# Two attention blocks side by side: 64-key half blocks, pads from the projection, and three relays through DRAM

## The chip, the cores and the metric

The kernel runs on one core of one Trainium2 chip. The metric is the device time of one execution, in microseconds (us). A program on one core has no second die to compare with, so "fast" here means within 1.5% of the fastest execution of the same kernel. The times are medians of all four executions of a run; four of these runs hold one slow execution (370.15, 420.29, 314.03 and 340.23 us; their fast executions alone give 369.87, 419.18, 313.94 and 339.91).

The profile's names: PE is TensorE (matmuls), PEld its weight loads, DVE is VectorE, ACT ScalarE, POOL GpSimd; SP is the engine that issues transfers (DMAs). PSUM is the memory that the matmuls of these kernels write to. The granted clock is the share of TensorE's full clock in the records.

## The reference

Two independent blocks of S = 2048 rows, D = 640, 32 heads of 20 columns. Block A is causal attention over a window of 256 keys. Block B is linear attention.

```python
qkv = (x @ wqkv).reshape(B, S, 3, H, Dh)...          # A
scores = einsum("bhqd,bhkd->bhqk", q, k) * Dh ** -0.5
mask = (i - j >= 0) & (i - j < 256)
a = softmax(where(mask, scores, -1e9)) @ v  -> @ wo
phi = lambda t: where(t > 0, t + 1, exp(t)) + 1e-6   # B
kv, z = phi(k)^T v, sum(phi(k))
b = (phi(q) kv) / (phi(q) z + 1e-6)  -> @ wo
return concatenate([a, b], axis=-1)                  # [1, 2048, 1280]
```

## The kernel before

A small planner in Python orders all operations by estimated times and emits them engine by engine. The order is then fixed. The SP queue issues nearly all transfers, in order.

A head has 20 columns, and the kernel gives each head a group of 32 rows (a pad). The old kernel projects 128 columns at a time, copies them to a stage, and moves each head's rows to its 32-row pad with a DMA of its own:

```python
def em(e, c=c):                                     # in proj_pad, for q and for k
    ...
    for h, r0, cnt, d0 in head_pieces[c]:           # 36 pieces per 512 queries
        hg, j = divmod(h, 4)
        nc.sync.dma_start(out=box["t"][32*j+d0 : 32*j+d0+cnt, hg, :],
                          in_=st["t"][r0 : r0+cnt, c, :])
```

One attention unit is 128 queries of 4 heads against 3 key blocks of 128. It takes 12 score matmuls, two exponentials, a mask multiply, and 12 matmuls in which the probabilities are stationary and 21 columns (20 values and a 1) move. The denominators come out in column 21, one per query, so VectorE divides with queries on the partitions, without any transfer:

```python
nc.vector.reciprocal(out=r[:], in_=O[:, :, Dh:HV])
nc.vector.tensor_tensor(out=otok..., in0=O[:, :, 0:Dh], in1=r[:].to_broadcast([P, 16, Dh]), op=ALU.mult)
```

Five transposes on TensorE then put the head columns on the partitions for the output projection.

The softmax here doesn't subtract the row's maximum and nothing guards it: scores larger than these inputs give would overflow.

Of the kernel before, what the change touches and what calls it, by code (L numbers as in the profile page):

```python
# [15 lines left out]
class Op:  # L16


    __slots__ = ("engs", "emit", "key", "left", "ready", "end", "succ", "lat", "group", "first", "last", "name")

    def __init__(self, engs, emit, key, lat, earliest):
        self.engs = engs
        self.emit = emit
        self.key = key
        self.lat = lat
        self.left = 0
        self.ready = earliest
        self.end = None
        self.succ = []
        self.group = None  # L30
        self.first = False
        self.last = False
        self.name = ""


class Planner:


    LAT = {"PE": 0.25, "ACT": 0.12, "DVE": 0.12, "POOL": 0.15, "SP": 2.2, "ACTQ": 2.2}

    def __init__(self, fill_bufs):
        self.avail = {}
        self.free = {}
        self.fill_bufs = fill_bufs
        self.fill_end = [0.0] * fill_bufs
        self.groups_open = 0
        self.n_groups = 0
        self.log = []

    def op(self, engs, emit, key, deps=(), lat=None, earliest=0.0, group=None, name=""):  # L50
        o = Op(engs, emit, key, lat, earliest)
        o.name = name or ".".join(emit.__qualname__.split(".<locals>.")[1:])
        o.group = group
        for d in deps:
            if d is None:
                continue
            if d.end is None:
                d.succ.append(o)
                o.left += 1
            else:  # L60
                o.ready = max(o.ready, d.end)
        if o.left == 0:
            self._push(o)
        return o

    def _push(self, o):
        for e in o.engs:
            self.avail.setdefault(e, []).append(o)

    def _start_time(self, o):  # L70
        if o.group is not None and o.first:
            return max(o.ready, self.fill_end[self.n_groups % self.fill_bufs])
        return o.ready

    def run(self):
        while True:
            best = None
            for e, ops in self.avail.items():
# [3 lines left out]
                t0 = INF  # L82
                for o in ops:
                    s = self._start_time(o)
                    if s < t0:
                        t0 = s
                if t0 == INF:
                    continue
                t = max(f, t0)
                pick = None  # L90
                for o in ops:
                    if self._start_time(o) <= t + 1e-9:
                        k = (o.key, o.ready)
                        if pick is None or k < pick[0]:
                            pick = (k, o)
                if best is None or t < best[0]:
                    best = (t, e, pick[1])
# [6 lines left out]
            if o.group is not None and o.first:  # L104
                slot = self.n_groups % self.fill_bufs
                o.group["slot"] = slot
                self.fill_end[slot] = INF
                self.n_groups += 1
# [4 lines left out]
            if o.group is not None and o.last:  # L113
                self.fill_end[o.group["slot"]] = o.end
# [5 lines left out]
        assert not any(self.avail.values())  # L120


def act_t(n):
    return 0.075 + 0.000833 * n


def dve_ps(n):
    return 0.07 + 0.00104 * n
# [11 lines left out]
def kernel(  # L140
# [14 lines left out]
    HD = 32  # L155
    HV = Dh + 1
    HG = H // 4
    KT = D // P
    NT = S // P
    NQ = 512  # L160
    NTT = S // NQ
    TB = NQ // P
    HALF = D // 2
    scale = float(Dh) ** -0.5
    out2 = out[0]
    xA = A_x[0]
    xB = B_x[0]
    PACE = 2.0
    EVK = -4000

    ctx.enter_context(tc.manual_schedule())
    pl = Planner(2)

    def pool(name, bufs, **kw):
        return ctx.enter_context(tc.tile_pool(name=name, bufs=bufs, **kw))

    PS = bass.MemoryType.PSUM
    const = pool("const", 1)
    wpool = pool("w", 1)
    xpool = pool("x", 4)  # L180
    stage_pool = pool("stage", 2)
    qpool = pool("q", 2)
    kpool = pool("k", 3)
    vpool = pool("v", 9)
    ppool = pool("p", 4)
    small = pool("small", 2)
    epool = pool("e", 3)
    opool = pool("o", 3)
    over = pool("over", 1)
    dram = pool("dram", 1, space=bass.MemoryType.DRAM)  # L190
    s3pool = pool("s3", 1, space=PS)
    s1pool = pool("s1", 2, space=PS)
    accpool = pool("acc", 1, space=PS)
    fpool = pool("fill", 2, space=PS)


    warm = const.tile([P, NQ], BF16, name="warm")
    nc.vector.memset(warm[:], 0.0)
    tiny = const.tile([P, 1], F32, name="tiny")
    nc.vector.memset(tiny[:], 1e-6)  # L200
    tinyo = const.tile([P, 1], F32, name="tinyo")
    nc.scalar.activation(out=tinyo[:], in_=tiny[:], func=ACT.Exp)
    ones = const.tile([P, 1], BF16, name="ones")
    nc.vector.memset(ones[:], 1.0)


    wA = [wpool.tile([P, KT, D], BF16, name=f"wA{i}") for i in range(3)]
    woA = wpool.tile([P, KT, D], BF16, name="woA")
    wkqB = pool("wkqB", 1)
    wvB = wpool.tile([P, KT, D], BF16, name="wvB")  # L210
    wo6 = wpool.tile([120, 6, D], BF16, name="wo6")
    wAv = A_wqkv.rearrange("(kt p) n -> p kt n", p=P)
    wBv = B_wqkv.rearrange("(kt p) n -> p kt n", p=P)

    MB = 1.0 / 0.2

    def dma(eng, emit, mbytes, key, deps=(), n=1, lat=2.2, name=""):
        return pl.op({eng: max(0.07 * n, mbytes * MB)}, emit, key, deps, lat=lat, name=name)

    def q_of(e):  # L220
        return nc.sync if e == "SP" else nc.scalar

    class Fifo:


        def __init__(self, n):
            self.n = n
            self.users = []

        def need(self):  # L230
            return self.users[-self.n] if len(self.users) >= self.n else []

        def add(self, ops):
            self.users.append(ops)


    x_users = Fifo(4)
    x_tiles = {}

    def load_x(which, t, key):  # L240
        src = (xA if which == "A" else xB).rearrange("s (c p) -> s c p", p=P)
        box = {}

        def emit(e, box=box):
            box["t"] = xpool.tile([P, KT, NQ], BF16, name="xT")
            for c in range(KT):
                nc.sync.dma_start_transpose(out=box["t"][:, c, :], in_=src[t * NQ : (t + 1) * NQ, c, :])  # L247

        o = dma("SP", emit, 0.655, key, deps=x_users.need(), n=5)
        box["op"] = o  # L250
        box["users"] = []
        x_users.add(box["users"])
        x_tiles[(which, t)] = box
        return box

    def load_w(eng, dst, src, key, mb=0.82, deps=()):
        return dma(eng, lambda e: q_of(eng).dma_start(out=dst, in_=src), mb, key, deps)


    def group(mms, evac, key, deps=(), shape=None, dtype=F32, chunk=2, name=""):  # L260

        g = {}
        name = name or mms[0][1].__qualname__.split(".<locals>.")[1]
        prev = None
        n = len(mms)
        i = 0
        first = True
        while i < n:
            part = mms[i : i + chunk]

            def emit(e, part=part, first=first):
                if first:
                    g["ps"] = fpool.tile(shape or [P, NQ], dtype, name="F")
                for _, m in part:
                    m(g["ps"])

            o = pl.op({"PE": sum(m[0] for m in part)}, emit, key if first else -1000, list(deps) if first else [prev], lat=0.0 if i + chunk < n else None, group=g, name=name)
            o.first = first
            if first:
                g["first"] = o  # L280
            prev = o
            first = False
            i += chunk
        g["mm"] = prev
        last = prev
        res = []
        for engs, em in evac:
            o = pl.op(engs, (lambda e, em=em: em(g["ps"], e)), EVK, [last], name=name)
            last = o
            res.append(o)  # L290
        last.group = g
        last.last = True
        g["ev"] = res
        g["end"] = last
        return g

    def copy_to(dst):
        def em(ps, e, dst=dst):
            d, s = dst(ps)
            if e == "ACT":  # L300
                nc.scalar.copy(out=d, in_=s)
            else:
                nc.vector.tensor_copy(out=d, in_=s)  # L303
        return em

    def either(n, act=True):
        d = {"DVE": dve_ps(n)}
        if act:
            d["ACT"] = act_t(n)
        return d  # L310

    head_pieces = []
    for c in range(KT):
        pieces = []
# [565 lines left out]
```

## Time and profile before

| | before |
|---|---|
| median of 3 runs before the prediction | 454.76 us |
| TensorE (PE) busy | 325.0 us, 72% |
| VectorE / ScalarE busy | 240.8 / 213.7 us |
| first score matmul | 67.55 us |
| pad transfers issued | 288 |

The first and fourth parts of the page follow: busy time by engine, then the shares of the chain of waits that ended last (SPq is the queue of SP; L370 is the pad transfer above).

```profile
span 452.2 us, 10028 instructions
PE 325.0 (72%) x4184; PEld 190.4 (42%) x4216; DVE 240.8 (53%) x478; ACT 213.7 (47%) x334; POOL 11.4 (3%) x36
...
PE 41%; SPq 22%; DVE 18%; ACT 7%; DMA 7%; issue 5%; DVEq 0%; ACTq 0%
```

The timeline at the start: start, duration, engine, line, operation, how many; in brackets, the idle time before it and what ended it.

```profile
15.29 27.67 SPq L370 DMA_DIRECT2D qpad<-stage  x36
...
43.06 16.34 SPq L370 DMA_DIRECT2D kpad<-stage  x22
...
64.80 2.83 PE L588 MATMUL F<-wkq,xT 128*128 128x320 bf16 x10 [35.50 <-DMA kpad<-stage]
```

An issue costs about 0.77 us (27.67 us for 36). All engines stand for 35 us behind the queue, and smaller holes of this kind follow at each new slice of 512 queries.

### The profile page before, as it was taken

The numbers are of one execution on the slowest core, as the hardware profiler recorded it, in microseconds if no ns is written. First come the engines' busy times: TensorE is split into PE (matmuls) and PEld (weight loads), VectorE is DVE, ScalarE is ACT, GpSimd is POOL, SyncE is SP. The second block draws the span as 40 slices with busy tenths as digits, with TensorE's granted clock in tenths as the row PEclk, the third lists the DMA queues.
The fourth block names the chain that finished last, engine by engine and source line by source line (L and its number), as shares of the span: only waits on it lengthen the run. The fifth ranks groups of instructions, "written<-read, shape, count | busy, mean of one in ns | idle before, by whom it ended". The sixth has DMA issues, their size and how long they took to land.

```text
span 452.2 us, 10028 instructions
## 1 busy us (share of the span) xinstructions
PE 325.0 (72%) x4184; PEld 190.4 (42%) x4216; DVE 240.8 (53%) x478; ACT 213.7 (47%) x334; POOL 11.4 (3%) x36
## 2 busy tenths in 40 slices
PE   5950025699945758899985789998771788797856
PEld 1430013255522426575653557545340444454523
DVE  0540006278742418766542437767741379779674
ACT  1000005288944539977102557898140598596020
POOL 4000000000000000000000005000000000000000
PEclk9895558599995559998996969699895799699898
DMA  9511133825254223370213133043111400010101
GB/s 217 130 25 24 25 95 74 150 55 105 50 154 91 50 54 79 64 141 20 66 27 81 25 86 64 2 105 97 39 26 36 111 15 16 17 61 17 58 30 58
DMA packets 62335, 29.82 MB, mean 66 GB/s; under 512 B 46546, under 2 KB 62162, under 8 KB 62290
## 3 DMA queue, kind: packets, MB, share of 16 engines
q1 hardware_dynamic: 60322, 27.55, 25.7%
q10 hardware_dynamic: 1968, 1.64, 1.2%
q8 instruction: 33, 0.54, 0.5%
q14 instruction: 12, 0.10, 0.1%
HBM read 9.99 MB, written 6.06 MB: 36 GB/s over the span
## 4 chain that ended last, share of the span: by engine, by line
PE 41%; SPq 22%; DVE 18%; ACT 7%; DMA 7%; issue 5%; DVEq 0%; ACTq 0%
SPq L370 17%; PE F L541 9%; PE F L346 7%; PE O L486 5%; PE F L620 5%; SPq L247 5%; DVE p L472 4%; DMA kpad<-stage 4%; ACT p L461 4%; PE F L388 3%; DVE rB L760 3%; DMA xT<-in_A_x_dram 2%; PE F L733 2%; DVE pq L575 2%; PE F L588 2%
## 5 line engine op out<-in xcount | busy, mean ns | idle before, releaser
L472 DVE TENSOR_TENSOR p<-p,maskED 128x1024 bf16<-128x1024 bf16 x112 | 77.4, 697 | 22.4 <-ACT p L464 21.9
L486 PEld LDWEIGHTS <-p 128*128 128x128 bf16 x1440 | 51.6, 98 | 32.1 <-DVE p L472 14.8
L486 PE MATMUL O<-v,p 128*128 128x21 bf16 x1440 | 57.2, 175 | 10.3 <-DVE p L472 6.6
L588 PE MATMUL F<-wkq,xT 128*128 128x320 bf16 x160 | 33.9, 341 | 36.7 <-DMA kpad<-stage 35.5
L444 PEld LDWEIGHTS <-kpad 20*128 20x128 bf16 x1440 | 25.6, 96 | 64.0 <-DMA kpad<-stage 32.6
L541 PE MATMUL F<-kvwo,pq 128*128 128x320 bf16 x160 | 32.4, 356 | 21.3 <-DVE osb L550 12.1
L550 DVE CAST osb<-F 128x320 bf16<-128x320 f32 x56 | 27.3, 489 | 35.0 <-PE F L541 17.6
L356 DVE CAST stage<-F 128x512 bf16<-128x512 f32 x32 | 22.1, 690 | 34.1 <-PE F L346 31.8
L346 PE MATMUL F<-xT,wA_115 128*128 128x512 bf16 x88 | 29.4, 442 | 14.2 <-DMA xT<-in_A_x_dram 12.3
L388 PE MATMUL F<-wA_117,xT 128*128 128x320 bf16 x160 | 33.3, 335 | 2.4 <-DVE osb L550 1.9
L588 PEld LDWEIGHTS <-xT 128*128 128x128 bf16 x160 | 15.3, 107 | 45.6 <-DMA kpad<-stage 35.8
L541 PEld LDWEIGHTS <-pq 128*128 128x128 bf16 x160 | 17.1, 112 | 33.0 <-issue 15.5
L541 PE MATMUL F<-woA,oT 128*128 128x320 bf16 x160 | 30.5, 316 | 0.3
L567 ACT ACTIVATE e_401<-F 128x320 bf16<-128x320 f32 x1 | 0.4, 437 | 64.0 <-PE F L588 64.0
L620 PE MATMUL F<-pk,xtok 128*128 128x320 bf16 x160 | 28.5, 316 | 0.0
L733 PE MATMUL F<-xT,wqp 128*128 128x512 bf16 x91 | 25.0, 383 | 4.0 <-DVE pq L575 2.9
L346 PE MATMUL F<-xT,wA_116 128*128 128x512 bf16 x91 | 24.0, 390 | 0.7 <-DVE GT L303 0.4
L400 DVE CAST v<-F 128x320 bf16<-128x320 f32 x28 | 13.8, 492 | 16.8 <-PE F L388 16.7
L388 PEld LDWEIGHTS <-xT 128*128 128x128 bf16 x160 | 15.5, 105 | 10.6 <-issue 2.9
L572 DVE TENSOR_SCALAR e_406<-e_401 128x320 bf16<-128x320 bf16 x1 | 0.2, 244 | 37.0 <-ACT e_401 L567 37.0
L346 PEld LDWEIGHTS <-wA_115 128*128 128x128 bf16 x100 | 9.3, 106 | 22.2 <-issue 11.8
L620 PEld LDWEIGHTS <-xtok 128*128 128x128 bf16 x160 | 14.8, 102 | 7.5 <-issue 0.2
(721 smaller groups left out, 537.1 us busy)
## 6 DMA issues: line engine op xcount, KB each, us to landing
out_dram<-osb SPq DMA_DIRECT2D x32, 160.0 KB
xtok<-in_B_x_dram SPq DMA_DIRECT2D x5, 512.0 KB
qpad<-stage SPq DMA_DIRECT2D x112, 20.0 KB
kpad<-stage SPq DMA_DIRECT2D x112, 20.0 KB
wkq<-in_B_wqkv_dram SPq DMA_DIRECT2D x2, 800.0 KB
wA_116<-in_A_wqkv_dram ACTq DMA_DIRECT2D x1, 800.0 KB
wA_117<-in_A_wqkv_dram SPq DMA_DIRECT2D x1, 800.0 KB
woA<-in_A_wo_dram SPq DMA_DIRECT2D x1, 800.0 KB
```

The costliest lines, as they stand in the source:

```text
L247: nc.sync.dma_start_transpose(out=box["t"][:, c, :], in_=src[t * NQ : (t + 1) * NQ, c, :])
L346: nc.tensor.matmul(ps[:], lhsT=wA[i][:, kt, c * P : (c + 1) * P], rhs=xb["t"][:, kt, :], start=(kt == 0), stop=(kt == KT - 1))
L370: nc.sync.dma_start(out=box["t"][HD * j + d0 : HD * j + d0 + cnt, hg, :], in_=st["t"][r0 : r0 + cnt, c, :])
L388: nc.tensor.matmul(ps[:], lhsT=xb["t"][:, kt, b * P : (b + 1) * P], rhs=wA[2][:, kt, hf * HALF : (hf + 1) * HALF], start=(kt == 0), stop=( ...
L444: nc.tensor.matmul(o, lhsT=kt_[HD * j : HD * j + Dh, hg, ko : ko + P], rhs=qbox["t"][HD * j : HD * j + Dh, hg, b * P : (b + 1) * P], start ...
L472: nc.vector.tensor_tensor(out=p[:, :, 0:3:2, :], in0=p[:, :, 0:3:2, :], in1=maskED[:, None, :, :].to_broadcast([P, 4, 2, P]), op=ALU.mult)
L486: nc.tensor.matmul(O[:, hh0 + j, 0:HV], lhsT=st["p"][:, j, i, :], rhs=vA[kb]["t"][:, hg * 4 + j, :], start=(i == idx0), stop=(i == 2))
L541: return lambda ps: nc.tensor.matmul(ps[:], lhsT=lhs(c), rhs=rhs(c, hf), start=(c == 0), stop=(c == KT - 1))
L550: nc.vector.tensor_copy(out=d, in_=ps[:])
L588: return lambda ps: nc.tensor.matmul(ps[:], lhsT=xb["t"][:, kt, b * P : (b + 1) * P], rhs=R["wk"][:, kt, hf * HALF : (hf + 1) * HALF], sta ...
L620: return lambda ps: nc.tensor.matmul(ps[:], lhsT=box["t"][:, tb, :], rhs=R["pk", tb // TB][:, tb % TB, hf * HALF : (hf + 1) * HALF], start ...
L733: return lambda ps: nc.tensor.matmul(ps[:], lhsT=R["wqp"][:, kt, c, :], rhs=xb["t"][:, kt, :], start=(kt == 0), stop=(kt == KT - 1))
```

## The change

The intent is to remove the pad DMAs and to make the attention cheaper:

- The weight columns are reordered on VectorE so that the projection gives 20 heads directly in 32-row pads. The 12 spare rows of each pad carry the columns of the other 12 heads, which are relaid through DRAM: 10 writes and 6 reads of 512 KB.
- Scores use 64-key halves with shifted query ranges, so that less masked-out work is done: 78 units of 2048 columns with one exponential each.
- The values become the stationary operand in 64x32 tiles, so the results have head columns on the partitions and need no transpose. The denominators now lie in one row per head. They go to DRAM, back as 128x32 for the reciprocal, to DRAM again, and back broadcast to 32 rows per head. Heads are then relaid through DRAM for the output projection.
- The planner is rewritten: PSUM banks by a common pool, scores paced, its own estimates of durations.

The core of the diff, cut; planner, pools, block B and the order of calls are left out:

```diff
-                for h, r0, cnt, d0 in head_pieces[c]:
-                    nc.sync.dma_start(out=box["t"][HD*j+d0 : HD*j+d0+cnt, hg, :], in_=st["t"][r0:r0+cnt, c, :])
+    def relay_write(m, tt, key):
+        dst = DQK[tt][0 : 32 * NH, :].rearrange("(r b) n -> b r n", b=NH)[4 * m : 4 * m + 4, :, :]
+        dma("SP", lambda q: q.dma_start(out=dst, in_=QK[m][:, c0 : c0 + RW]), 0.52, ...)
+    def relay_read(g, tt, key):
+        src = bass.AP(..., ap=[[NH * RW, 4], [RW, 32], [1, RW]])
+        dma("SP", lambda q: q.dma_start(out=QK[g][:, c0 : c0 + RW], in_=src), 0.52, ...)
 ...
-                    nc.tensor.matmul(O[:, hh0 + j, 0:HV], lhsT=st["p"][:, j, i, :], rhs=vA[kb]["t"][:, hg * 4 + j, :], ...)
+                        nc.tensor.matmul(FB[box[rg]][32*j : 32*j+32, qc : qc+w], lhsT=V[...][64*rho : 64*rho+64, HV*h : HV*h+32],
+                                         rhs=PT[u % NP][64*rho : 64*rho+64, j, cc : cc+w], ..., tile_position=(64*rho, 32*j))
 ...
-                nc.vector.reciprocal(out=r[:], in_=O[:, :, Dh:HV])
+        dma("SP", lambda q: q.dma_start(out=d1[:], in_=ON[nb][Dh : Dh + 97 : 32, :]), ...)
+        dma("SP", lambda q: q.dma_start(out=RC[nb][:], in_=d1[:].rearrange("a (b c) -> (a b) c", c=32)), ...)
+        pl.op({"DVE": 0.35}, lambda e: nc.vector.reciprocal(out=RD[nb][:], in_=RC[nb][:]), ...)
+        dma("SP", lambda q: q.dma_start(out=d2[:].rearrange("a (b c) -> (a b) c", c=32), in_=RD[nb][:]), ...)
+        dma("SP", lambda q: q.dma_start(out=RB[nb][:], in_=d2[:, None, :].to_broadcast([4, 32, TQ])), 0.3, ..., lat=2.6)
+        # OS = ON * RB on VectorE, then:
+            dst = DO[tt][:].rearrange("(r b) n -> b r n", b=32)[4 * g : 4 * g + 4, :, :]     # g < 5
+            dst = DO[tt][o : o + P, :]                                                         # g >= 5
+        dma("SP", lambda q: q.dma_start(out=dst, in_=os_[:]), 0.26, ...)
+            src = DO[tt][:].rearrange("(r b) n -> b r n", b=32)[4 * m : 4 * m + 4, :, :]
+            dma("SP", lambda q, m=m, src=src: q.dma_start(out=OT[:, m, :], in_=src), 0.26, ...)
```

## The prediction

> **What bounds the kernel now.** The span is 452.2 us (the page's first part) with PE busy 325.0 (72%), DVE 240.8, ACT 213.7. In a table of 10 us windows PE is busy 9 to 9.9 of 10 wherever it is fed (90 to 120, 190 to 230, 270 to 310); the other 127 us are holes. The largest is 29.9 to 64.8: no compute engine works, and the list of waits gives PE 35.5 us on the last kpad transfer. The chain of waits gives 22% to the SP queue, 17% of it the line that relays heads into 32-row pads. The timeline shows why: 36 such issues last 27.67 us, 0.77 each, and there are 288 (DMA issues: 224 full pieces, 64 part pieces), about 220 us of one in-order queue. Holes at 130 to 170, 230 to 270 and 330 to 360 end on the same transfers. So: SP issues at each new 512-query slice, otherwise PE.
>
> **Removed.** The 288 pad issues. 128 score units with two exponentials each (1.13 us for 1152 columns, 0.48 for 384: about 196 us of ACT). Attention on PE: scores about 50 us, values 57 us busy (group table). Mask multiplies 77.4+6.5 us DVE, transposes 7.3 PE and 7.7 DVE, four wide reciprocals 13.4.
>
> **Added or moved.** 78 units of 2048 columns: the slope of the measured exponentials (0.84 ns a column) gives 1.88 us each, 147 in all. Masks shrink to 61,440 columns, about 40 us. I count 1600 score and 2144 value matmuls, in 32x64 and 64x32 tiles. Today's 12 four-tile score matmuls start within 0.14 us and the next full-array one 0.14 us after the last of them; this agrees with the Trainium skill, "TensorEngine Tiling (Array Packing)", Key Properties: tiles run in parallel, a change of mode drains the array. At about 16 ns per matmul plus some 190 mode changes at 0.1 us I estimate 60 to 70 us of attention on PE, 40 less than now. ACT and DVE gain copies (B's projections before phi, 32 of 512 columns for the value sums) and 32 normalisations of about 0.6 us. DMA grows from 29.8 to about 47 MB (pads through DRAM 8.4, reciprocals broadcast 8.4, heads through DRAM 5.2), with five dependent SP issues for each of 16 head groups, each link about 2 us (a pad lands in 1.9 today).
>
> **On the critical path.** PE work becomes about 278 us. At today's share where fed, 0.92, that is 302; a start of about 12 without the pad stall and a tail of about 8 (last denominators, rows and store) give about 320. ACT and DVE need about 195 us each if shared evenly, so they do not bound.
>
> **Predicted: 318 us, 8 times in 10 between 288 and 362.** Faster by over 2%: 0.96; within 2%: 0.02; slower: 0.02.
>
> **Signs.** Right if: no hole over 10 us after the first 20; first score unit before 20 us; PE busy 260 to 295 us and over 80% of the span; exponentials about 1.88 us x78; SP queue under 10% of the chain; granted clock above 0.9 (holes show 0.5). Wrong if PE busy stays above 310 (small tiles issue slower than 16 ns), or SP waits on its own DRAM round trips dominate.
>
> **What could make it wrong.** Head-of-line blocking in SP: transposing loads still take 1.26 us each, 60 of them, and denominator round trips wait in the same queue. If landing takes 4 us rather than 2 the plan slips, and 350 or more is likely. If the new schedule fits the engines' true times well, 290.

## The result, and the profile after

The changed kernel takes 471.34 us (median of 4 runs, 469.85 to 471.66), the old one 455.44 in the same rounds. The ratio is 1.035, 95% interval 1.030 to 1.040: slower. Ratios here are the mean time of one kernel's fast runs over that of the other's in the same rounds, so they are not quite the ratio of the medians.

The same parts of the page after the change (the second line of shares goes by source line), and the line of its DMA part for the SP queue:

```profile
span 470.0 us, 11365 instructions
PE 305.6 (65%) x5000; PEld 166.6 (35%) x5000; DVE 221.4 (47%) x442; ACT 191.5 (41%) x168; POOL 128.8 (27%) x155
...
q1 hardware_dynamic: 60858, 40.97, 54.2%
...
DMA 53%; PE 19%; DVE 12%; SPq 10%; issue 4%; ACT 1%; POOL 0%; POOLq 0%; DVEq 0%; ACTq 0%
DMA RB<-d 22%; DMA RC<-d 8%; DMA d<-RD 8%; SPq L355 7%; DMA d<-ON 6%; PE F L657 3%; PE F L622 3%; PE F L424 3%; DVE OS L602 3%; DMA OT<-do 3%; DMA do<-OS 3%; PE F L394 3%; PE F L726 2%; PE SC L483 2%; PE F L572 2%
```

Three engines have less work, as intended: PE 19 us less, VectorE 19, ScalarE 22. (GpSimd has 117 us more, since it takes most of the masks.) But transfers hold 53% of the chain where they held 7%. The broadcast of the reciprocals (RB<-d) alone has 22%, and the four links of the denominators together about 43%. The list of waits for VectorE says the same: engine, tile, line, what it waited for; total, times, longest.

```profile
DVE OS L602 <- DMA RB<-d: 97.8, 13, 21.9
DVE RD L596 <- DMA RC<-d: 36.9, 9, 10.4
```

How that stops everything is seen in the timeline at 300 us:

```profile
299.77 1.15 SPq L598 DMA_DIRECT2D RB<-d  x1
300.97 5.33 SPq L355 DMA_TRANSPOSE X<-in_B_x_dram  x1
306.35 0.57 SPq L594 DMA_DIRECT2D d<-ON  x1
314.61 0.69 DVE L602 TENSOR_TENSOR OS<-ON,RB 128x512 bf16<-128x512 f32 x1 [21.86 <-DMA RB<-d]
315.22 0.68 DVE L317 CAST R<-F 128x512 bf16<-128x512 f32 x1
...
315.94 0.63 ACT L648 ACTIVATE E<-R 128x512 bf16<-128x512 bf16 x1 [20.24 <-DVE R L317]
315.96 0.58 PE L726 MATMUL F<-X,XT 128*128 128x512 bf16 x1 [21.30 <-DVE R L317]
```

The broadcast is issued at 299.77 and VectorE starts on it at 314.61. In the planned order of VectorE the normalisation stands in front of the copy that frees a PSUM bank (R<-F), and VectorE starts that copy only afterwards. So ScalarE and PE wait for a transfer that neither of them reads. The table of windows shows two stretches of 10 us without any work (busy time of PE, weight loads, VectorE, ScalarE and GpSimd, then granted clock, share of the 16 DMA engines, GB/s):

```profile
110.00:120.00 10.00, 0.00 (x0) 0.00 (x0) 0.00 (x0) 0.00 (x0) 0.00 (x0) 0.50 0.94 97
...
300.00:310.00 10.00, 0.00 (x0) 0.00 (x0) 0.00 (x0) 0.00 (x0) 0.00 (x0) 0.50 0.89 116
```

The share of 0.94 does not mean that 16 engines moved data. It adds up the durations of packets, the parts of a transfer that the trace records. In the first of these stretches 26 of 1908 packets took over 0.5 us each and hold 95.7 of the 150.5 us; 22 of the 26 are of 256 bytes or less, and the usual packet of 256 bytes takes 18 ns. So that time was waiting for the most part.

Why does a transfer of 512 KB take so long? The trace records every update of a semaphore by a DMA. The Trainium skill ("DMA: Bandwidth & Descriptors", Why a DMA increments its semaphore by 16 and not by 1) says that a transfer from the SP queue runs on k of 16 DMA engines, k being the largest number up to 16 that divides the outermost dimension (the slowest one that is not 1) on both sides. By the same section each of the k engines posts one update, and the issuer posts the rest at once. The count of updates per transfer therefore tells k: 16 for k = 16, otherwise k + 1. Counted from the records of the changed kernel (landing is from the end of issue to the last update, the median of the transfers whose records are complete):

```
transfer                       size     x    updates  engines  landing, median us
RB<-d    broadcast             512 KB   16   5        4        8.7
dqk<-QK  pad relay, write      512 KB   10   5        4        10.5
QK<-dqk  pad relay, read       512 KB    6   5        4        14.7
OT<-do   head relay, read      256 KB   10   5        4        9.0
do<-OS   head relay, g < 5     256 KB   10   5        4        6.5
do<-OS   head relay, g >= 5    256 KB    6   16       16       2.1
out      stores (POOL queue)   160 KB   32   16       16       1.5 to 2.3
X<-B_x   transposing loads               40   16       16       5.7  (2.1 in the old kernel)
```

A few transfers lack an update or more in the records; the counts are the usual ones. In the old kernel pads of 20 rows show 11 updates, so 10 engines. The packets say the same without the rule: for most of the time in which a broadcast moves, exactly four of its packets of 4 KB are in flight, 159 ns each. So 128 packets need about 5.1 us on four engines (an estimate), and the fastest broadcasts land in 7.4.

The page also says that it is always the lowest-numbered k engines. If that holds, 22 of the 50.3 MB (16, 10 and 6 times 512 KB, 20 times 256 KB) go through the same 4 engines, which also carry their share of everything else. At 4 KB in 159 ns these 22 MB alone keep four engines busy for about 213 us (an estimate).

**Theory A:** the outermost dimension of 4 confines these transfers to 4 engines, which clogs them for all other traffic; the dependent denominators then wait in that jam. **Rival B:** the number of dependent round trips in one in-order queue costs the time, whatever their bytes. **Rival C:** a large transfer by itself, or reading the same DRAM rows 32 times, is slow.

### The profile page after: what moved, and what is told of

The parts are those of the page before. It is cut to its first block, busy times and chain, and to the rows that moved or that the text cites. A ratio compares the mean times of both kernels' runs of the same rounds, so it can differ in the third digit from the quotient of the medians.

```text
span 470.0 us, 11365 instructions
## 1 busy us (share of the span) xinstructions
PE 305.6 (65%) x5000; PEld 166.6 (35%) x5000; DVE 221.4 (47%) x442; ACT 191.5 (41%) x168; POOL 128.8 (27%) x155
## 4 chain that ended last, share of the span: by engine, by line
DMA 53%; PE 19%; DVE 12%; SPq 10%; issue 4%; ACT 1%; POOL 0%; POOLq 0%; DVEq 0%; ACTq 0%
DMA RB<-d 22%; DMA RC<-d 8%; DMA d<-RD 8%; SPq L355 7%; DMA d<-ON 6%; PE F L657 3%; PE F L622 3%; PE F L424 3%; DVE OS L602 3%; DMA OT<-do 3%; DMA do<-OS 3%; PE F L394 3%; PE F L726 2%; PE SC L483 2%; PE F L572 2%
## 5 line engine op out<-in xcount | busy, mean ns | idle before, releaser
L490 ACT ACTIVATE P<-SC 128x2048 bf16<-128x2048 f32 x78 | 146.4, 1877 | 144.9 <-PE SC L483 143.7
L513 POOL TENSOR_TENSOR P<-P,MK 128x512 bf16<-128x512 bf16 (+1 forms) x94 | 99.7, 1068 | 276.2 <-ACT P L490 272.0
L602 DVE TENSOR_TENSOR OS<-ON,RB 128x512 bf16<-128x512 f32 x32 | 23.2, 744 | 102.0 <-DMA RB<-d 97.8
L657 PE MATMUL F<-W,X 128*128 128x320 bf16 x160 | 30.5, 343 | 41.1 <-DVE R L317 36.8
L726 PE MATMUL F<-X,XT 128*128 128x512 bf16 x100 | 28.5, 424 | 27.4 <-DVE R L317 24.1
L572 PE MATMUL F<-P,V 64*32 64x64 bf16 (+4 forms) x2144 | 31.8, 254 | 21.2 <-issue 13.1
L622 PE MATMUL F<-W,OT 128*128 128x320 bf16 x160 | 30.1, 340 | 22.6 <-DMA OT<-do 16.0
L483 PE MATMUL SC<-QK 20*64 20x128 bf16 (+4 forms) x1600 | 36.6, 272 | 4.8 <-ACT P L490 3.1
L317 DVE CAST R<-F 128x320 bf16<-128x320 f32 (+1 forms) x55 | 28.2, 521 | 13.1 <-PE F L622 5.6
L666 PE MATMUL F<-R,XT 128*128 128x320 bf16 x160 | 27.2, 321 | 1.6 <-DVE ON L317 1.6
L513 DVE TENSOR_TENSOR P<-P,MK 128x512 bf16<-128x512 bf16 (+1 forms) x54 | 25.7, 482 | 3.7 <-ACT P L490 3.4
```

The source lines that it names most:

```text
L317: nc.vector.tensor_copy(out=dst, in_=src)
L483: nc.tensor.matmul(SC[64 * rho : 64 * rho + 64, j, cc : cc + w], lhsT=QK[g][32 * j : 32 * j + Dh, kc : kc + 64], rhs=QK[g][32 * j : 32 * j ...
L490: nc.scalar.activation(out=pt[:], in_=SC[:], func=ACT.Exp, scale=scale)
L513: eng.tensor_tensor(out=pt[:, :, cc : cc + w], in0=pt[:, :, cc : cc + w], in1=MK[:, None, lo:hi].to_broadcast([P, 4, w]), op=ALU.mult)
L572: nc.tensor.matmul(FB[box[rg]][32 * j : 32 * j + 32, qc : qc + w], lhsT=V[kb % NV][64 * rho : 64 * rho + 64, HV * h : HV * h + 32], rhs=PT ...
L602: pl.op({"DVE": dve_ps(NX)}, lambda e, c=c: nc.vector.tensor_tensor(out=os_[:, c], in0=ON[nb][:, c], in1=RB[nb][:, c], op=ALU.mult), -2900 ...
```

## The experiments

Eleven experiments in twelve runs, each timed in rounds with the old kernel. The changed kernel is the base unless said otherwise.

### All five kinds on 16 engines

Each transfer is cut into four of 32 rows. Bytes and planned order stay.

```diff
-q.dma_start(out=RB[nb][:], in_=d2[:, None, :].to_broadcast([4, 32, TQ]))
+for j in range(4):
+    q.dma_start(out=RB[nb][32*j : 32*j+32, :], in_=d2[j : j+1, :].to_broadcast([32, TQ]))
-q.dma_start(out=dst, in_=QK[m][:, c0 : c0 + RW])
+for j in range(4):
+    q.dma_start(out=dst[j], in_=QK[m][32*j : 32*j+32, c0 : c0 + RW])
 # and likewise QK<-dqk, do<-OS for g < 5, OT<-do
```

> Same plan and same bytes as the changed kernel; each transfer whose outermost dimension is 4 (reciprocal broadcast, pad relay both ways, head relay both ways) is cut into four of 32 rows. Theory A (those transfers run on 4 of the 16 engines and clog them for all others): every one now shows all engines, the 512 KB broadcast lands in about 3 us after its issue instead of 8.7, span 300 to 350 us. Rival B (the dependent chain of round trips in one in-order queue costs, whatever the bytes): 150 more issues at 0.5 us in that queue, span unchanged or worse, 460 to 500 us.

370.15 us, ratio to the old kernel 0.815 (0.809 to 0.820), result correct. Rival B falls as the reason for these 100 us, since there are more issues and the same links; what the links cost with all engines is measured further below. A's number was missed: 370 is outside 300 to 350. One of the four executions, the profiled one, took 1340 us (see the last section), so the kernel was run again.

> The kernel with all transfers on 16 engines once more, because the profile of its first run fell in an execution of 1340 us with matmuls four times as long. 368 to 372 us, and a usable profile: PE busy about 305 us, no hole over 10 us after the first 30.

369.52 us, ratio 0.814. The shares of the chain, first by engine and then by line:

```profile
span 369.0 us, 11580 instructions
...
PE 32%; DVE 24%; DMA 21%; SPq 14%; issue 5%; ACT 2%; POOL 0%; DVEq 0%; POOLq 0%; ACTq 0%
DMA RB<-d 9%; PE F L394 7%; PE F L432 5%; SPq L355 5%; DVE OS L614 5%; PE F L680 4%; SPq L608 4%; PE F L645 4%; PE SC L491 3%; DVE R L673 3%; DMA RC<-d 3%; PE F L580 3%; DVE R L317 3%; DVE P L521 3%; SPq L634 3%
```

Each piece now shows 16 updates, and up to about 16 packets of the broadcast are in flight. One piece of it (128 KB) lands in 2.6 us. The whole broadcast, from the end of its first issue to the landing of its fourth piece, takes 4.3 us (was 8.7) and not the 3 expected; the pad relays take 4.5 and 5.0 (10.5 and 14.7). Five head reads together take 11.6 us where they took 15.6: their 20 pieces land 0.45 us apart, and one issue takes 0.42. The transposing loads of block B, which the edit does not touch, land in 1.6 us (5.7): they had been waiting behind the others. PE busy was expected at about 305 us; it is 282.2 in this profile. "No hole over 10 us" was just missed: PE has one of 10.7 us at 230 us.

### One part at a time

> Only the broadcast of the reciprocals is cut into four of 32 rows; the relays stay on 4 engines. A: broadcast lands in 3 to 5 us, about half of the gain of the run with all cut, span 370 to 420 us, since 13.6 MB still go through 4 engines. B: unchanged, 465 to 480.

Only the broadcast cut by rows: 431.88 us, ratio 0.952, a gain of 39 us and less than expected. The whole broadcast lands in 5.0 us (median), at the end of what was expected. But the relays are still on 4 engines (the pad relays land in 9.7 and 15.3 us), and other links land later than with all cut (d<-RD in 2.7 us, not 1.1).

> The reverse: pad and head relays are cut into 32 rows, the broadcast stays on 4 engines (8.4 MB). A: x transposes land faster (median 5.7 us falls towards 2.1), broadcast alone takes about 8 us still, span 390 to 430 us. B: unchanged or worse, 465 to 490.

Only the relays cut: 412.52 us, ratio 0.910, a gain of 59 us. Transposing loads land in 2.4 us, the broadcast still takes 8.2. The two gains add up to 98 us; both cuts together give 101. (The old kernel's medians in the rounds of these runs, 452.39 to 455.44 us, allow such differences to within some 3 us.)

### Controls for the cut itself

```diff
+for j in range(4):                                       # e4: by columns, outermost still 4
+    q.dma_start(out=RB[nb][:, 256*j : 256*j+256], in_=d2[:, None, 256*j : 256*j+256].to_broadcast([4, 32, 256]))
+for j in range(2):                                       # e9: by rows, outermost 2
+    q.dma_start(out=RB[nb][64*j : 64*j+64, :], in_=d2[2*j : 2*j+2, None, :].to_broadcast([2, 32, TQ]))
```

> Control: the broadcast is cut into four DMAs by columns, each still with an outermost dimension of 4, so the same number of issues as the row cut but the same 4 engines. A: no gain, 465 to 490 us, last piece lands as late as before. A rival C, that one large DMA is slow and several in flight are faster, expects the gain of the row cut here too (under 430).

475.58 us, ratio 1.046: no gain from the cut as such, although four transfers are in flight. Each piece shows 5 updates. The pieces land one after the other, 1.4 us apart, and the last comes 8.6 us after the end of the first issue (one broadcast: 8.7).

> The changed kernel with the broadcast cut into two DMAs whose outermost dimension is 2: 256 KB each, same bytes. Theory A in its sharp form (the outermost dimension sets how many engines a transfer gets, and they are the same few each time): 2 engines, 3 updates per landing, 512 KB land in about 16 us after issue, span clearly longer than 471, 530 to 620 us. Rival (a transfer is slow because it is large, or because it reads the same DRAM rows 32 times): no longer than the changed kernel, 455 to 480.

547.47 us, ratio 1.203. Each piece shows 3 updates, so 2 engines. While both pieces are under way mostly two packets are in flight, not four, and the second lands 5.0 us (median) after the first: both go through the same two engines. The broadcast takes more of the chain than in any other run:

```profile
span 547.4 us, 11386 instructions
...
DMA 57%; PE 17%; issue 8%; SPq 8%; DVE 8%; ACT 1%; POOL 0%; POOLq 0%; DVEq 0%
DMA RB<-d 30%; DMA d<-RD 8%; DMA d<-ON 6%; DMA RC<-d 5%; SPq L355 4%; PE F L394 3%; DVE OS L606 3%; DMA OT<-do 2%; PE F L626 2%; PE F L661 2%; PE F L424 2%; PE SC L483 2%; PE F L572 2%; SPq L600 2%; DMA W<-in_A_wo_dram 1%
```

The same bytes in smaller transfers cost 76 us more. Rival C falls with these two: size and repeated reads are as before, or smaller. The sharp form of A stands, the outermost dimension setting the engines. The landing of 16 us after the issue was an overestimate: both pieces together take 13.3 us (median of 16; 11.8 to 19.0).

### The same links without the bytes

```diff
-q.dma_start(out=RB[nb][:], in_=d2[:, None, :].to_broadcast([4, 32, TQ]))
+q.dma_start(out=RB[nb][0:P:32, :], in_=d2[:])            # wrong result on purpose
```

> Wrong result on purpose. In the changed kernel as it is, the broadcast moves only the 4 rows of 4 KB and not their 32 copies: all five dependent links, the issues and the plan stay, 8.1 MB on 4 engines go. Theory A: 425 to 440 us, as with the broadcast on 16 engines (432). Rival B (number of links): no change, 465 to 475.

420.29 us, ratio 0.925. The links, the issues and the plan are unchanged, and 51 us go with the 8.1 MB. This is a little more than expected, and 12 us more than when the broadcast runs on all engines.

### What remained: the plan and the chain

370 is still 52 us over the prediction. Two candidates: the planner believes that a cut transfer takes one issue when it takes four (`n=4` corrects it), or the chain of the denominators itself.

> The same, and the planner is told that these transfers take four issues each, so that it orders the SP queue by their true cost. If what is left over 318 us is an in-order queue that runs late against its plan, 345 to 362 us. If the queue is no longer the limit, 366 to 374.

350.63 us, ratio 0.771: the true issue counts were worth 19 us. The normalisations' waits for the broadcast, 97.8 us in the changed kernel and 38.5 with all engines, are gone from the list of waits.

> Wrong result on purpose. With all transfers on 16 engines, the denominator chain of the 16 head groups is taken out: the normalisation multiplies by ones that were set at the start. What is left of the chain's latency and of its SP waits goes away. If the remaining 50 us over my prediction are that chain: 315 to 335 us. If they are PE work, masks and copies: 355 to 368.

314.03 us, ratio 0.691 (wrong result), just under the first case. Against 369.5 with the same issue estimates, the chain costs 55 us, with all engines at work. But leaving out operations also lets the planner order the rest anew, so the test was repeated with the informed plan.

> Wrong result on purpose. The chain is taken out of the version with all engines and the informed plan (350.6 us), so that both sides of the comparison order their queue with true issue counts. If the chain itself costs about 36 us there, 308 to 318 us. If the informed plan had already hidden most of it and the earlier run without a chain gained by a luckier order, 325 to 345.

318.22 us, ratio 0.699 (wrong result), at the upper edge of the first case. So with true issue counts the chain costs 32 us (350.6 to 318.2), what the planner gains by its absence included, and without it the true counts are worth nothing (314 and 318). The page's first part of the informed plan, and then of the same without the chain:

```profile
span 348.4 us, 11567 instructions
PE 279.5 (80%) x5000; PEld 160.4 (46%) x5000; DVE 238.0 (68%) x457; ACT 189.2 (54%) x164; POOL 117.9 (34%) x144
```

```profile
span 315.8 us, 11364 instructions
PE 267.8 (85%) x5000; PEld 154.1 (49%) x5000; DVE 234.5 (74%) x444; ACT 188.8 (60%) x163; POOL 118.8 (38%) x143
```

From the lists of waits: the normalisation with all engines (369.5 us), then the score matmuls and the reciprocal with the informed plan, then the score matmuls without the chain.

```profile
DVE OS L614 <- DMA RB<-d: 38.5, 9, 11.2
...
PE SC L491 <- ACT P L498: 20.1, 17, 2.1
DVE RD L604 <- DMA RC<-d: 9.6, 6, 3.8
...
PE SC L492 <- ACT P L499: 2.2, 5, 1.1
```

### A faster version

The informed plan with all engines, and the denominators moved directly from their four rows to the 128x32 tile, without DRAM: one link fewer.

```diff
-q.dma_start(out=d1[:], in_=ON[nb][Dh : Dh + 97 : 32, :])
-q.dma_start(out=RC[nb][:], in_=d1[:].rearrange("a (b c) -> (a b) c", c=32))
+q.dma_start(out=RC[nb][:], in_=ON[nb][Dh : Dh + 97 : 32, :].rearrange("a (b c) -> a b c", c=32))
```

> A faster version from the one with all engines and the informed plan (350.6): the denominators go from the ON rows straight to the 128x32 tile, without DRAM, one of four links less. If what is left of the chain's cost (about 36 us over the run without a chain) is its links: 338 to 346. If it is bytes or other queues: 348 to 353.

340.23 us, ratio 0.747 (0.742 to 0.752), correct: the best correct version, 25% under the old kernel.

> The same with reciprocals in bf16, so that the broadcast moves half: 4.2 MB less. If the bytes still matter with all engines at work (DMA share about 0.5): another 5 to 10 us off. If only links do: within 2 us of the version before it.

342.70 us, ratio 0.753. Half the bytes of the broadcast bring nothing once 16 engines carry them. That points to links, issues and the plan's order as what is left; no run tells these apart.

## Why the prediction was wrong

It gave 318 us with 96% for faster; measured were 471 us and slower by 3.5%. Point by point:

- **The bound of the old kernel.** The holes and the pad issues were read from its timeline. No run here tested that reading. The changed kernel has no pad issues, and its first score matmul comes at 27.3 us, not 67.6. "Before 20 us" was too early: the timeline has PE waiting 4.1 us for the value weights just before that.
- **Work on the engines: right.** Exponentials: 78 of 1.877 us (predicted 1.88). Attention on PE: 36.6 + 31.8 us busy in the group table (predicted 60 to 70). The signs of tiles running in parallel and draining at a change of mode, which the Trainium skill states ("TensorEngine Tiling (Array Packing)", Key Properties), gave a usable estimate. The mask multiplies were estimated at about 40 us of VectorE, but the plan gave 94 of 148 to GpSimd at 1.07 us each, 99.7 us busy; the ones on VectorE cost 0.48 us. PE busy is 305.6 us, over the 260 to 295 of the signs, at a granted clock of 0.783; without the jam it is 279.5 and 267.8 us.
- **The step that failed: "with five dependent SP issues for each of 16 head groups, each link about 2 us".** The 2 us came from a 20 KB pad on 10 engines and was put on a 512 KB broadcast. The links were costed by count, and the 47 MB by their sum, never by how many engines each transfer would get. That could have been read from the diff: an outermost dimension of 4 stands in five places. The same page of the Trainium skill says it under Rules for kernel authors, "Use all 16 engines", and gives a leading zero-stride broadcast as the example (here the 4 leads, and the stride of zero stands second). In its place the runs show 8.7 us for the broadcast, 4.9 us (median) even for the first link of 16 KB, which stands behind others, and 102 us gained (471 to 369.5) when the same bytes go over all engines.
- **"A tail of about 8" as the chain's only share of the critical path: wrong too.** In the changed kernel the normalisations stand in VectorE's order before copies that PE waits for, and wait 97.8 us for the broadcast. Even with all engines and a plan that knows its issues, the chain costs 32 us, and how is open: the normalisations no longer wait there. Against the run without the chain PE is busy 12 us longer (279.5 and 267.8, at granted clocks of 0.894 and 0.956) and idle 21 us longer; 18 of these are longer waits of score matmuls for exponentials (20.1 and 2.2 us), which the plan's new order may cause as well as the links.
- **What could make it wrong.** The text named late landings and gave "350 or more". The direction was right, the weight far too small: a range up to 362 held no jam of this size.
- The version without the chain takes 318.2 us, the number predicted. That is partly luck: its first score matmul came at 26.5 us, 14.5 later than assumed, so other terms were too large by about as much. PE was busy 267.8 us where the sum had 278, and no tail of denominators was left.

What stays open: the trace does not record which four engines were used. That transfers under way together share the same ones is seen in the packets: with five head reads of the changed kernel under way, about four packets are in flight, and the reads land one after the other, 2.6 us apart; with two pieces on 2 engines, two. That it is the same four throughout the kernel is inferred, also from untouched 16-engine loads landing 3.5 times later while those transfers run (5.7 against 1.6 us).

## What to carry to other kernels

Before costing a transfer by its bytes, look at the outermost dimension of both its sides: it sets how many DMA engines carry it, and here 52 such transfers slowed the others too. Count the semaphore updates per transfer in a trace to see it, and cut by rows, not by columns, to mend it. A wait for a transfer must not stand, in an engine's fixed order, in front of the copies that free PSUM, or its latency becomes TensorE's; and a planner must know the true number of issues.

## What the Trainium skill lacked or had wrong

- "DMA: Bandwidth & Descriptors", Why a DMA increments its semaphore by 16 and not by 1, and Rules for kernel authors: the rule on the number of engines is there, and the runs agree with it for k = 2, 4, 10 and 16 (3, 5, 11 and 16 updates). What it lacks is the price of ignoring it for others: 16-engine transposing loads landed in 5.7 us beside 4-engine transfers and in 1.6 us without them, and the kernel took 471 us instead of 369.5.
- The same page, Specifications, names about 27 GiB/s for each engine (29 GB/s). The packets of the broadcast come near it: 4 KB in 159 ns, 25.8 GB/s. Over a whole broadcast, 8.0 us from issue in the fastest cases of the chain, it is 16 GB/s for each of four engines with all fixed costs included; the page has no figure for such a read.
- "TensorE: Matmul & The Clock Gate", Part 1, warns that the activity records are unreliable and that the clock has been seen stuck at a quarter for 50 us and more. Here one execution of 1340 us out of four of the same kernel recorded a granted clock of 1.000 throughout, with PE busy 99% and the 320-column output matmuls at 1199 ns each (326 ns in the repeat). A quarter of the clock would fit times that are 3.7 times as long, but the records do not show it. It did not come back in the repeat; its cause is open.
